# A fused attention and gated-linear kernel: three tiles' down products in one group, and stores, reloads and weight transfers placed anew

## The chip, the cores and the metric

The kernel runs on one core of a Trainium2 chip. A core has five instruction streams that run side by side and wait for one another by semaphores: TensorE (PE, with its weight loads shown apart as PEld), VectorE (DVE), ScalarE (ACT), GpSimd (POOL) and SyncE (SP). Each works through its own instructions in order. In this kernel nearly all transfers are issued by SP. The metric is the device time of one execution in microseconds; the time given is the median of several runs. One execution was also recorded by the hardware profiler; all rows quoted here come from such records, with times counted from the start of its span.

## The reference

The input x has 2048 rows of 512. Two blocks follow one another, each with a layer norm whose scale and shift come from a conditioning vector, and a gate on its result:

```python
x = x + ga * attention(layernorm(x) * (1 + ca) + sa)      # 32 heads, 4 segments of 512 rows, a memory from segment to segment
h = layernorm(x) * (1 + cb) + sb
g = h @ w_gate                                            # 512 x 1376
u = h @ w_up                                              # 512 x 1376
x = x + gb * ((g * u) @ w_down)                           # 1376 x 512
```

The change touches only the second block. The 1376 columns of g and u make eleven tiles: ten of 128 columns (numbers 0 to 9) and one of 96 (number 10, called LAST).

## The kernel before

The kernel works in single-precision inputs split into a high and a low part, so that a product takes three matmuls: high by high, low by high, high by low. In the code a pair of such parts is bH and bL (activations), cwH and cwL (gate and up weights), dH and dL (down weights), mH and mL (the product g * u). High parts are made by ACT with a copy, low parts by DVE with a subtraction.

The rows come in four segments of 512. The second block takes them in two passes: pass 0 has segments 0 and 1, pass 1 has segments 2 and 3. Within a pass the two segments are c = 0 and c = 1, and a segment has four row tiles t = 0 to 3.

**Two ways to do a tile.** Tiles 0, 1 and LAST of pass 0, and LAST of pass 1, are *plain*: `open0` multiplies the first half of the contraction for segment 0 (banks Xg and Xu) and keeps a copy q on ACT, `close0` adds the second half, and `other` does segment 1 (banks Yg and Yu), adding q to it. The other tiles go in pairs as *units*, one for g and one for u, which do a two-by-two block product with seven block multiplications instead of eight; their banks are X, Y and Z, and `build` prepares the sums of activation blocks that they need. `finish` takes what comes out: a copy gs on ACT for g, and for u the product on DVE followed by `split`, which makes mH on ACT and mL on DVE.

**Down products.** `down(p, fs, c, t)` multiplies the tiles in `fs` with their rows of w_down into one bank, acc, three matmuls to a tile, and adds the bank to the row tile xa on DVE (line 1344). For the tiles whose first is `ENDS[p]` the row tile is then complete: `down` issues its store to the output at once, and, in pass 0, the *reload* of the same buffer with the rows that pass 1 needs, at most three stores behind. `d` takes one down product out of the list `dq`; in the loop over units it is called between the steps of a unit, to give PE work while the others catch up.

**Kept weights.** Pass 0 loads and splits the weights of each tile and stores the split parts to device memory (`keep`, line 406); pass 1 fetches them (`fetch`, line 410) and has ACT copy them in place (line 416). `prepare(n)` is the generator that gets unit n's weights ready two units ahead. It is advanced step by step inside unit n - 1 (`old`), and for kept units started at step 4 of unit n - 2 (`pr`). There it fetches cwH and cwL; the fetches of the two down tiles come as later steps of the same generator, behind ACT's copies.

**What sets the order.** PE's instructions are chained in the order of the program. The other engines' orders come from a scheduler that works with its own estimate of times, so the order on ACT, DVE and SP can shift when the program order does. SP issues transfers in its order, and an issue whose buffer or data is not ready holds those behind it.

The stretch from the first plain tile to the unit loop is written out by hand, near the end of the kernel. `lg1` is the layer norm of segment 1; its last four steps are the 16 transposes of the normed rows (ctp) with ACT's scale and shift (chf, line 611). `xp`, `wdp` and `pr0` are the weights of tile LAST, the three plain down tiles (whose splits dHp and dLp share one buffer) and unit 0.

## Time and profile before

| | |
|---|---|
| time, median of 3 runs | 880.75 us (878.02 to 881.43) |
| the profiled execution's own time | 879.9 us |
| its span | 878.2 us |
| PE busy | 845.7 us, 96% |
| DVE busy | 655.6 us, 75% |
| ACT busy | 496.6 us, 57% |
| POOL busy | 274.4 us, 31%, nothing after about 520 us |
| moved by DMA | 141.29 MB, mean 161 GB/s |

The first block takes the span up to about 520 us; the plain tiles of pass 0 stand from 520 to 565, the units of pass 0 up to about 690, LAST of pass 1 up to about 706, and the units of pass 1 up to the end. A row of the timeline reads: start, length, engine, line, operation, output and inputs, shapes, count, and in brackets the idle time of the engine just before it with what ended it. Matmuls overlap and their ends are modelled, so that the distance from start to start says what one costs.

### The profile page before, as it was taken

To read this page: it belongs to the slowest core of one execution; us is meant where nothing else is said; L and a number is where in the kernel's file an instruction comes from. 1 tells how busy PE (TensorE), PEld (TensorE's weight loads), DVE (VectorE), ACT (ScalarE), POOL (GpSimd) and SP (SyncE) were. 2 spreads that over 40 slices of the span, in tenths; PEclk is the share of its full clock that TensorE was granted. 3 is DMA by queue.
4 is the path that set the end of the run, shared out by engine and by line. 5 is a ranking of instruction groups with operands and counts; after the bars stand their busy time and mean duration, and the time that the engine had idled before them with its cause. 6 is when DMAs were issued, how large, how long until landed. Compare 5 with 4: busy or idle time off the path is not lost.

```text
span 878.2 us, 14439 instructions
## 1 busy us (share of the span) xinstructions
PE 845.7 (96%) x4976; PEld 596.4 (68%) x4976; DVE 655.6 (75%) x1825; ACT 496.6 (57%) x755; POOL 274.4 (31%) x424
## 2 busy tenths in 40 slices
PE   8989999999999999999999999999999999999998
PEld 5755666565665565665665677877888777888886
DVE  7698777888778887788889358989796935546654
ACT  3757757677677685677544626343535745554420
POOL 4545535466546574575424610000000000000000
PEclk9999999999999999999999999999999999999999
DMA  7554443545536453557465448477742576342112
GB/s 236 154 162 123 122 120 100 172 129 172 132 88 184 119 149 113 132 165 227 147 202 188 143 167 311 162 247 281 254 178 84 199 240 229 148 175 89 49 49 96
DMA packets 83305, 141.29 MB, mean 161 GB/s; under 512 B 11712, under 2 KB 45504, under 8 KB 83232
## 3 DMA queue, kind: packets, MB, share of 16 engines
q1 hardware_dynamic: 83088, 140.35, 50.4%
q8 instruction: 39, 0.64, 0.3%
q14 instruction: 34, 0.28, 0.1%
q10 hardware_dynamic: 144, 0.02, 0.0%
HBM read 90.52 MB, written 49.55 MB: 160 GB/s over the span
## 4 chain that ended last, share of the span: by engine, by line
PE 75%; DVE 12%; ACT 6%; DMA 4%; issue 2%; POOL 1%; SPq 0%; ACTq 0%; POOLq 0%; DVEq 0%
PE acc L1341 14%; PE tb L85 8%; PE q L85 6%; PE k L85 6%; PE Xu L1274 5%; PE Xg L1274 5%; DVE q L39 5%; PE wops L85 5%; PE vps L85 4%; PE Yu L1274 4%; PE Yg L1274 4%; PE kps L85 3%; PE qps L85 3%; ACT pt L332 2%; PE Zu L1274 1%
## 5 line engine op out<-in xcount | busy, mean ns | idle before, releaser
L39 DVE CUSTOM_DVE_ANT_0 q<-q,cmask 128x384 f32<-128x384 f32 (+3 forms) x512 | 246.6, 508 | 49.7 <-PE q L85 39.6
L332 ACT ACTIVATE pt<-k 128x1024 f32<-128x1024 f32 x160 | 163.8, 1024 | 64.4 <-PE k L85 63.7
L338 POOL TENSOR_SCALAR_AFFINE_SELECT pt<-pt 128x256 f32<-128x256 f32 (+1 forms) x224 | 96.8, 446 | 166.1 <-ACT pt L332 163.7
L85 PE MATMUL q<-kst,qst 96*128 96x384 bf16 (+3 forms) x512 | 101.6, 299 | 11.4 <-DVE nm L39 9.8
L85 PE MATMUL k<-qst,kst 98*128 98x384 bf16 (+3 forms) x512 | 97.1, 302 | 5.0 <-ACT pt L332 4.9
L1344 DVE TENSOR_TENSOR xa<-xa,acc 128x512 f32<-128x512 f32 x96 | 65.6, 684 | 38.9 <-PE acc L1341 38.5
L85 PE MATMUL tb<-pt,v 128*32 128x512 f32 (+3 forms) x1024 | 75.5, 436 | 0.0
L39 DVE DVE_READ_ACCUMULATOR2_ANT nm<- 128x1 f32 x512 | 72.3, 141 | 0.0
L85 PEld LDWEIGHTS <-kst 98*128 98x128 bf16 x512 | 37.7, 98 | 49.5 <-issue 43.2
L85 PEld LDWEIGHTS <-qst 96*128 96x128 bf16 x512 | 43.1, 97 | 37.9 <-issue 14.1
L1341 PE MATMUL acc<-dH,mL 128*128 128x512 f32 (+1 forms) x152 | 60.0, 395 | 1.3 <-DVE mL L1294 1.3
L1341 PE MATMUL acc<-dH,mH 128*128 128x512 f32 (+1 forms) x152 | 60.3, 397 | 0.0
L1341 PE MATMUL acc<-dL,mH 128*128 128x512 f32 (+1 forms) x152 | 60.1, 395 | 0.0
L85 PEld LDWEIGHTS tb<-pt,v 128*32 128x32 f32 x1024 | 28.7, 109 | 38.6 <-issue 33.8
L364 ACT ACTIVATE tsb<-tb 128x512 f32<-128x512 f32 x32 | 19.0, 595 | 41.0 <-PE tb L85 41.0
L1341 PEld LDWEIGHTS acc<-dH,mL 128*128 128x128 f32 (+1 forms) x152 | 28.5, 188 | 8.4 <-DVE mL L1294 1.7
L1341 PEld LDWEIGHTS acc<-dL,mH 128*128 128x128 f32 (+1 forms) x152 | 28.6, 188 | 7.0
L1341 PEld LDWEIGHTS acc<-dH,mH 128*128 128x128 f32 (+1 forms) x152 | 28.5, 188 | 6.8
L1274 PE MATMUL Xu<-bH,cwH 128*128 128x512 f32 (+1 forms) x68 | 27.7, 407 | 3.2 <-DVE yu L1374 1.7
L85 PE MATMUL kps<-ahH,wkH 128*128 128x512 f32 x64 | 30.0, 469 | 0.0
L85 PE MATMUL wops<-woH,oH 128*128 128x512 f32 x64 | 28.3, 441 | 0.7 <-ACT oH L527 0.7
L85 PE MATMUL qps<-ahH,wqH 128*128 128x512 f32 x64 | 28.7, 448 | 0.0
(378 smaller groups left out, 2034.3 us busy)
## 6 DMA issues: line engine op xcount, KB each, us to landing
wm<-in_w_mod_dram SPq DMA_DIRECT2D x24, 256.0 KB, 4.4
kd<-k SPq DMA_DIRECT2D x16, 384.0 KB, 2.5
kst<-kd SPq DMA_DIRECT2D x32, 192.0 KB, 3.2
qd<-q SPq DMA_DIRECT2D x16, 384.0 KB, 3.1
qst<-qd SPq DMA_DIRECT2D x32, 192.0 KB, 3.6
x<-in_x_dram SPq DMA_DIRECT2D x16, 256.0 KB, 4.5
kst<-kd SPq DMA_DIRECT2D x32, 128.0 KB, 3.1
qst<-qd SPq DMA_DIRECT2D x32, 128.0 KB, 3.7
```

Of the source, the lines that this page charges most:

```text
L39: i = getattr(self.eng, name)(*a, **k)
L85: return pe(nc.tensor.matmul(*a, **k))
L332: ex = act.activation(pt, kp, AF.Exp, scale=0.25)
L338: sels[u, i] = nc.gpsimd.affine_select(w, w, pattern=[[0, w.shape[1]], [1, P]], compare_op=ALU.is_ge, fill=0.0, base=0, channel_multiplier=-1)
L364: act.activation(tsbs[u], tbs.pop(u), AF.Copy)
L1274: pe(nc.tensor.matmul(ps[0:n], a, b[:, k], start=first and c == 0, stop=last and c == 5, skip_group_check=True))
L1341: pe(nc.tensor.matmul(ps, a[0:m, t * P:(t + 1) * P], b[0:m], start=j == 0, stop=j == n - 1))
L1344: vec.tensor_add(xa, xa, ps)
```

## The change

There are four edits.

1. The down products of the plain tiles of pass 0 were two groups for each row tile, (0, 1) and (LAST,), thus two banks and two additions. They become one group `trio = (LAST, 0, 1)` of nine matmuls and one addition. For segment 0 the four groups stand together after `close0(0, LAST)`; for segment 1 four entries instead of eight go into `dq`, and unit 0 takes them at steps 1, 2, 4 and 6.
2. `run(lg1)`, segment 1's transposes, moves from after `close0(0, 0)` to after `open0(0, LAST)`; the first steps of `build` and of the down weights shift with it.
3. The store of a finished row tile of pass 0 is not issued by the down product that completes it but by the next one that does, and the reload that follows from it is later by as much. The first down product of pass 1 issues what is left.
4. For units with kept weights `prepare` issues all transfers (cwH, cwL, and for a u unit both pairs of down tiles; for the plain tile of pass 1 also its down tile) in its first step. ACT's copies follow step by step as before.

```diff
     def down(p, fs, c, t):
+        while p == 1 and outs and fs[0] != ENDS[1]:
+            store(0)
         while p == 1 and again:
             reload()
...
         if fs[0] == ENDS[p]:
-            nc.sync.dma_start(out[rows(2 * p + c, t), :], xa)
-            if p == 0:
-                again.append((c, t))
+            outs.append((c, t, xa))
+            if p == 1:
+                store(p)
+            else:
+                if len(outs) > 1:
+                    store(p)
                 if len(again) > 2:
                     reload()
+
+    outs = []
+
+    def store(p):
+        c, t, xa = outs.pop(0)
+        nc.sync.dma_start(out[rows(2 * p + c, t), :], xa)
+        if p == 0:
+            again.append((c, t))
...
         slot = -n % 3
+        if (nm, i) in wkeep:
+            gens = [(xprep if nm == "x" else wprep)(n, slot, pc, pc)]
+            gens += [wdprep(p, f) for f in {"g": (), "u": (i, i + 1), "x": (LAST,)}[nm]]
+            for g in gens:
+                next(g)
+            yield
+            for g in gens:
+                yield from g
+            return
...
     run(close0(0, 0))
-    run(lg1)
-    nb = build(0)
-    next(nb)
-    run(close0(0, 1))
     for w in wdp[:2]:
         next(w)
+    run(close0(0, 1))
     run(open0(0, LAST, qa[LAST]))
+    run(lg1)
     for w in wdp[:2]:
         next(w)
     next(wdp[2])
-    next(nb)
-    for t in range(2):
-        down(0, (0, 1), 0, t)
+    nb = build(0)
     next(nb)
     run(close0(0, LAST))
+    next(wdp[2])
     next(nb)
-    for t in range(2, 4):
-        down(0, (0, 1), 0, t)
+    trio = (LAST, 0, 1)
     for t in range(4):
         xload2(0, 1, t)
+    for t in range(4):
+        if t == 2:
+            next(nb)
+        down(0, trio, 0, t)
...
+    next(nb)
     for _ in other(0, LAST):
         next(pr0)
...
     for f in (0, 1):
-        for t in (2 * f, 2 * f + 1):
-            down(0, (LAST,), 0, t)
         for _ in other(0, f):
...
-    dq.extend(lambda f=f, t=t: down(0, f, 1, t) for f in ((LAST,), (0, 1)) for t in range(4))
+    dq.extend(lambda t=t: down(0, trio, 1, t) for t in range(4))
...
             if n == 0:
-                d(1 + st % 2 if st > 1 else 1)
+                d(st in (1, 2, 4, 6))
```

## The prediction

> **What bounds the kernel now.** I read the page first, then PE's waits over the second half, then the PE, ACT, DVE and SP timelines around each wait.

> ```profile
> span 878.2 us, 14439 instructions
> PE 845.7 (96%) x4976; PEld 596.4 (68%) x4976; DVE 655.6 (75%) x1825; ACT 496.6 (57%) x755; POOL 274.4 (31%) x424
> ```

> PE is busy for 96% of the span, and the change leaves every matmul in place: the compiled order has the same PE instructions in both kernels, and nothing in it differs ahead of the feed-forward part, at about 520 us. So only PE's pauses after 520 us can move. The PE timeline, where a bracket gives the idle time and its releaser, has these (rows from five places):

> ```profile
> 537.16 0.51 PE L1341 MATMUL acc<-dHp,mH 128*128 128x512 f32 x1 [0.51 <-ACT mH L1293]
> 537.89 0.51 PE L1341 MATMUL acc<-dHp,mL 128*128 128x512 f32 x1 [0.22 <-DVE mL L1294]
> 592.50 0.50 PE L1274 MATMUL Xu<-bH,cwH 128*128 128x512 f32 x1 [1.28 <-DVE yu L1374]
> 603.36 0.50 PE L1341 MATMUL acc<-dH,mL 128*128 128x512 f32 x1 [1.26 <-DVE mL L1294]
> 735.39 0.50 PE L1274 MATMUL Xu<-bH,cwH 128*128 128x512 f32 x1 [0.45 <-DVE yu L1374]
> 741.30 0.50 PE L1274 MATMUL Xu<-bH,cwH 128*128 128x512 f32 x1 [1.49 <-DVE p5u L1374]
> ```

> The brackets sum to 5.2 us. A bracket starts at the modelled end of the last matmul, which lies about 0.17 us after the next could have started, so each pause costs about that more: 1.2, 1.45, 1.45, 0.6 and 1.65 us, 6.3 us in all, 0.7% of the span. That is the ceiling of any gain, since the tail is untouched. A change under 0.5% (4.4 us) is about what a measurement of this kernel cannot tell from none, and the three runs shown spread by 3.4 us.

> **Part 1: grouping, and the transposes moved.** Eight down groups fewer mean eight DVE additions fewer, from this row 8 x 0.68 = 5.5 us of DVE.

> ```profile
> L1344 DVE TENSOR_TENSOR xa<-xa,acc 128x512 f32<-128x512 f32 x96 | 65.6, 684 | 38.9 <-PE acc L1341 38.5
> ```

> This is worth nothing in itself: its own idle time says that DVE waits 38.5 us for PE around these additions, and the two pauses that DVE does set after it, at 592 and 603 us, start from work that the change does not thin out. From the third weight split on (about 581 us) the DVE and ACT orders are alike in both kernels, and before it DVE waits for PE again:

> ```profile
> 586.39 0.69 DVE L1374 TENSOR_TENSOR p1u<-Zu,p1u 128x512 f32<-128x512 f32 x1 [1.23 <-ACT p1u L1394]
> 591.77 0.68 DVE L1374 TENSOR_TENSOR yu<-Xu,yu 128x512 f32<-128x512 f32 x1
> ```

> So DVE has no backlog at 586 us that fewer additions could shorten, and between 586 and 592 us it runs splits and products queued ahead of yu. I keep both pauses: 0.

> What costs is the order ahead of the first down product. Before, two down groups of tiles 0 and 1 stand between tile 2's two halves (open0 and close0 of LAST). After, the compiled order of PE is open0 of LAST, 16 transposes, close0 of LAST, then at once the grouped down products, which begin with LAST, the tile just finished. Nothing stands between to cover LAST's product and split. Rows for PE and ACT:

> ```profile
> 525.83 0.39 PE L1274 MATMUL Xg<-bh,gH 128*128 128x512 f32 x1
> 528.56 1.91 PE L88 MATMUL ctp<-ident,x 128*128 128x128 f32 x16
> 530.22 0.48 PE L1274 MATMUL Xg<-bh,gH 128*128 128x512 f32 x1
> ...
> 530.39 1.44 ACT L611 ACTIVATE chf<-ctp,modc 128x512 f32<-128x512 f32 x2
> 531.72 0.63 ACT L1310 ACTIVATE dHp<-crd 128x512 fp32r<-128x512 f32 x1
> 533.43 0.63 ACT L1230 ACTIVATE bH<-t 128x512 fp32r<-128x512 f32 x1
> 533.95 0.59 ACT L1365 ACTIVATE gs<-Xg 128x512 f32<-128x512 f32 x1
> 536.00 0.59 ACT L1441 ACTIVATE q<-Xu 96x512 f32<-96x512 f32 x1
> 536.49 0.62 ACT L1293 ACTIVATE mH<-gs 128x512 fp32r<-128x512 f32 x1
> 537.14 0.69 DVE L1294 TENSOR_TENSOR mL<-gs,mH 128x512 fp32r<-128x512 f32 x1 [0.94 <-ACT mH L1293]
> 542.91 0.68 DVE L1370 TENSOR_TENSOR gs<-gs,Xu 96x512 f32<-96x512 f32 x1 [0.54 <-ACT cwH L479]
> 563.10 1.29 DVE L1238 TENSOR_TENSOR t<-chf,chf 128x512 f32<-128x512 f32 x2
> ```

> Twelve matmuls take 2.73 us (525.83 to 528.56), the 16 transposes 1.66 (528.56 to 530.22). In the new order: close0 of tile 0 ends at 528.56, of tile 1 at 531.29, open0 of LAST at 534.02, the transposes at 535.68, close0 of LAST at 538.5 (0.1 for the restart after transposes). ACT, in its new order, copies the last open0 result until 534.75 (0.2 after its end, 0.53 to the next, as at 536.00), then has four chf (0.67 each, 1.33 for two in the row), one dHp (0.53), two bH (0.52 each) and only then the gate copy gs, at 539.0. The copy takes 0.6, the product on DVE 0.7, mH 0.65 with its handover: PE may start at 541.1. The low half mL follows 0.7 later, as 537.16 to 537.89 shows, against a matmul's 0.23, another 0.5. PE pauses 2.6 + 0.5 = 3.1 us where it paused 1.2. Cost 1.8. The ends: with ACT's copy of gs done early, Xu's end, product and mH alone leave 1.6 + 0.5, cost 0.9; with DVE slips of one more 0.6 us operation, 2.5. I take 1.8, because ACT's order is fixed and every link has a row.

> Later, at about 566 us, the six Y groups of 2.7 us now follow one another without down products between. DVE has 28 operations there, at 0.6 from start to start (the row at 563.10) under 16.8 us, and four of them are half as wide; PE needs 16.4 us, so DVE keeps up; the last tile's mL comes 0.7 us behind mH as above, with two thirds of the first grouped product (1.4 us) and a Z group (1.4 us) ahead of it. From Y's end: addition 0.7, mL of tile 0 0.6, product 0.6, mH 0.65, mL 0.7, or 3.25 us against 3.0 of cover: cost 0.25, from 0 to 1.

> **Part 2: kept transfers together, stores and reloads later.** The last two pauses begin on ACT, which waits in order for transfers that SP issued late:

> ```profile
> 724.54 0.69 DVE L1344 TENSOR_TENSOR xa<-xa,acc 128x512 f32<-128x512 f32 x1 [2.07 <-PE acc L1341]
> 722.88 0.38 SPq L1346 DMA_DIRECT2D out_dram<-xa  x1
> 726.55 0.38 SPq L410 DMA_DIRECT2D dH<-keptHd  x1
> 727.50 0.38 SPq L1346 DMA_DIRECT2D out_dram<-xa  x1
> 732.44 0.32 SPq L1321 DMA_DIRECT2D xa<-x1d  x1
> 732.87 0.37 SPq L410 DMA_DIRECT2D cwH<-keptHu  x1
> 731.11 0.63 ACT L416 ACTIVATE dH<-dH 128x512 fp32r<-128x512 f32 x1 [4.51 <-DMA dH<-keptHd]
> 734.65 0.69 DVE L1374 TENSOR_TENSOR yu<-Xu,yu 128x512 f32<-128x512 f32 x1
> 737.60 1.79 ACT L416 ACTIVATE cwH<-cwH 128x1024 fp32r<-128x1024 f32 x2 [3.70 <-DMA cwH<-keptHu]
> 740.56 0.68 DVE L1374 TENSOR_TENSOR p5u<-Xu,p5u 128x512 f32<-128x512 f32 x1
> 741.50 0.58 ACT L1394 ACTIVATE p5g<-Yg 128x512 f32<-128x512 f32 x1
> xa<-x1d SPq DMA_DIRECT2D x1, 256.0 KB, 9.9
> ```

> (The last row is the issue at 711.80, which stood behind two 896 KB fetches; its last column is us to landing.) SP sat from 727.50 to 732.44 on a reload whose store had not landed, with cwH queued behind it. In the new SP order the first pair of kept down tiles (dH, dL of tile 2) moves ahead of the second store, out of the way. Three of the last reloads come first, then dH and dL of tiles 3 and 4, the store, cwL and cwH, and the reload last.

> SP is the only queue touched; POOL and ACT issue none of these. At the first tiles SP also changes the order of stores of split weights, the second rows' x and one weight fetch; each is wanted 15 us or more after its issue, so 0.

> dH 3 is free when the last first-half product ends on PE (724.5), and the store ahead of it now follows its addition, not two reloads, so I put its issue at 724.9, not 726.55, and its landing 4.5 later at 729.4. ACT's gate copy, mH and the yu copy behind it follow 1.7 us sooner, yu on DVE at about 733, and PE is not held at 734.8: gain 0.6.

> The cw pair is issued when its slot comes free on PE (727.9) instead of at 732.9, 5 us sooner, but behind four down tiles and now with cwL first: I estimate cwH at 728.3 + 4.7 (its time alone, 732.9 to 737.6) + 2.7 for cwL (4.7 less a latency of 2) + 0.5 for what is left of the tiles, 736.2 against 737.6. Also mH of the waiting product now stands ahead of cwH in ACT's order. Then p5u need not wait for it, and the pause of 1.65 goes, as far as ACT is through with cwH and cwL (twice 1.79) and p5g by 740.4, when PE wants its bank. (Unheld, PE starts Xu at 734.8; Xu, Yg and Xg of 1.4 each bring it to the Xu that needs p5u at 739.05, and one more to 740.4.) 736.2 + 3.6 + 0.5 is 740.3. What is late next is thus ACT itself, and after it the last reload: its addition now stands directly ahead of p5u on DVE. Bounds of this part: gain 2.25, or a loss of 2.0 (below); I take a gain of 1.9, near the first, since issue times move only to the earlier side.

> Later kept units have the same SP, ACT and DVE order in both kernels and PE has no pause there; the tail is the same. The sum: +1.8 + 0.25 - 1.9 = +0.15 us on the profiled run's 879.9, which stands 0.85 under the median of 880.75. So 880.9 for a median.

> **Rivals.** *The clock falls in the new pause.* PE lost half its clock early in this run after a wait of 2.0 us and a stretch of one-column matmuls, and kept it after the 1.49 us wait at 741:

> ```profile
> 17.54 1.05 PE L85 MATMUL m<-ones,wm 128*128 128x1 f32 x8 [2.00 <-DVE wm L39]
> 19.00:20.00 1.00, 1.00 (x8) 0.86 (x7) 0.97 (x4) 0.00 (x0) 0.00 (x0) 0.83 0.00 0
> 20.00:21.00 1.00, 1.00 (x4) 0.81 (x3) 0.09 (x2) 0.79 (x2) 0.00 (x0) 0.50 0.42 129
> 23.00:24.00 1.00, 1.00 (x5) 0.58 (x3) 1.00 (x2) 0.73 (x3) 0.00 (x0) 0.96 0.00 0
> 741.00:744.00 3.00, 2.70 (x12) 2.22 (x13) 2.27 (x5) 2.64 (x5) 0.00 (x0) 1.00 0.10 27
> ```

> (In the windows the third number from the end is the granted clock.) The new pause of 2.6 us, one matmul, 0.5 us lies above the first wait. There the clock was halved from inside the slice at 19 to inside that at 23, some 3.4 us; the same here loses half of it, 1.7 us: 882.6. [...]

> *Slower: the last reload blocks DVE.* It is issued once its store has landed, about 732, behind cwL and cwH. If it takes the 9.9 us of the row above it lands at 741.9; the addition and p5u follow to 743.3, and PE, which wants p5u's bank at 739.05, pauses 4.25 us where it paused 2.25: Part 2 then costs 2.0 and the sum is 880.75 + 1.8 + 0.25 + 2.0 = 884.8. It decides from a landing at about 738; with a landing past 742.2, or with the clock's 1.7 beside it, the time passes 885.15, the 0.5% bound. Against it: the 9.9 us row was issued 1.3 us behind the pair, this reload would be 4 us behind. I expect 737.

> *Faster: the backlog argument is wrong,* and the DVE time saved removes the pauses at 592 and 603 (2.9 us), with Part 1 at its low end (0.9) and Part 2 at 2.25: 880.75 + 0.9 - 2.9 - 2.25 = 876.5; with another microsecond it would pass 876.35.

> *No effect in Part 2:* dH and cwH land no earlier because the four down tiles share the engines; then +2.05, 882.8.

> **Numbers.** Sum as worked out 0.45; half clock 0.2; no gain in Part 2 0.13; reload blocks 0.12; faster 0.1. The first three lie within 0.5%. Of the reload case I count all as slower, since a landing that late would likely be later still, and add 0.02 from the clock; of the faster case 0.08 as faster and 0.02 as within: 0.78, 0.14, 0.08. The range runs from the faster case's edge to a little past the reload case: 877 to 886. The likeliest case alone: 879 to 882.6.

> **What will show it.** PE's first matmul of the grouped product (acc from LAST's mH) should carry a bracket of about 2.4 us, its second 0.2 to 0.3. At about 594 and 605 the waits for yu and mL should stand as they do. At about 737 and 743 PE's waits for yu and p5u should be gone or under 0.5. Additions xa should be 88. The prediction fails if PE's first grouped product starts without a wait, if the granted clock in that stretch is 0.5, or if DVE's longest wait before p5u is for a transfer of xa.

## The result, and the profile after

In 20 runs of each on one chip the changed kernel took 882.59 us (881.06 to 884.24) and the kernel before 879.66 us (876.61 to 882.19): a ratio of 1.0034, with a 95% interval of 1.0025 to 1.0044. That is 3.0 us more, inside the 0.5% within which the prediction said "no change", but clear of zero: with 20 runs of each, a third of a per cent can be told from none. The page of the profiled execution, whose own time was 883.86 us:

```profile
span 882.1 us, 14432 instructions
PE 849.2 (96%) x4976; PEld 599.9 (68%) x4976; DVE 652.5 (74%) x1817; ACT 497.1 (56%) x755; POOL 274.6 (31%) x424
```

PE has the same 4976 matmuls and is busy 3.5 us longer, DVE has its eight operations fewer. How much of it lies in the feed-forward part is seen in the PE timeline, from the first gate product to the last down product. The first pair of rows is of the kernel before, the second of the changed one:

```profile
520.37 0.39 PE L1274 MATMUL Xg<-bh,gH 128*128 128x512 f32 x1
873.90 0.40 PE L1341 MATMUL acc<-dL,mH 128*128 128x512 f32 x1
```

```profile
521.03 0.39 PE L1274 MATMUL Xg<-bh,gH 128*128 128x512 f32 x1
877.88 0.40 PE L1343 MATMUL acc<-dL,mH 128*128 128x512 f32 x1
```

353.53 us became 356.85, 3.3 us more. This length is used below beside the medians, since it leaves out the attention part, which varies from execution to execution. Where it was lost, in PE's timeline of the changed kernel (rows from five places):

```profile
541.80 0.51 PE L1343 MATMUL acc<-dHp,mH 96*128 96x512 f32 x1 [2.50 <-ACT mH L1293]
542.52 0.58 PE L1343 MATMUL acc<-dHp,mL 96*128 96x512 f32 x1 [0.22 <-DVE mL L1294]
542.89 0.63 PE L1343 MATMUL acc<-dLp,mH 96*128 96x512 f32 x1
543.32 0.63 PE L1343 MATMUL acc<-dHp,mH 128*128 128x512 f32 x1
...
546.26 0.40 PE L1343 MATMUL acc<-dHp,mL 96*128 96x512 f32 x1
...
572.19 0.49 PE L1343 MATMUL acc<-dHp,mH 128*128 128x512 f32 x1 [0.29 <-ACT mH L1293]
572.91 0.50 PE L1343 MATMUL acc<-dHp,mL 128*128 128x512 f32 x1 [0.23 <-DVE mL L1294]
...
597.72 0.50 PE L1274 MATMUL Xu<-bH,cwH 128*128 128x512 f32 x1 [1.28 <-DVE yu L1387]
608.56 0.50 PE L1343 MATMUL acc<-dH,mL 128*128 128x512 f32 x1 [1.27 <-DVE mL L1294]
744.50 0.50 PE L1274 MATMUL Xu<-bH,cwH 128*128 128x512 f32 x1 [0.23 <-DVE p5u L1387]
746.46 0.50 PE L1274 MATMUL Yg<-bH,cwH 128*128 128x512 f32 x1 [0.30 <-ACT p5g L1407]
```

Two things are to be seen at 542 us. The first is a stand, a time in which PE starts nothing, of 2.50 and 0.22 us in brackets. The second has no bracket: from 542.89 to 546.26 us eight matmuls take 3.37 us, 0.42 each and not 0.23. Windows of the same trace, with PE's busy time first and the granted clock as the third number from the end:

```profile
539.40:542.80 3.40, 0.79 (x2) 0.47 (x3) 2.71 (x5) 2.45 (x6) 0.00 (x0) 1.00 1.05 404
542.80:546.20 3.40, 3.40 (x9) 2.63 (x9) 0.94 (x3) 0.81 (x2) 0.00 (x0) 0.50 0.70 255
546.20:549.60 3.40, 3.40 (x16) 2.77 (x16) 3.09 (x6) 0.00 (x0) 0.00 (x0) 1.00 0.00 0
```

PE did 9 matmuls in 3.4 us at half clock, where it does 16 at full clock.

The table sums, place by place, how much later than 0.2275 us after its forerunner each matmul started (0.1 us after a transpose; differences under 0.04 us left out). It is worked out from the PE timelines of each profiled execution, and has all the kernels of the next section. "Ahead of the first group" is the stretch from 535 to 548 us, half clock included; the fillers of e3 and e10 (1.8 and 0.9 us of matmuls) are work and not in it.

| kernel | ahead of the first group | about 570 us | about 593 and 604 us | about 735 to 748 us | from first gate product to last matmul |
|---|---|---|---|---|---|
| before | 1.28 | 0 | 3.2 | 2.47 | 353.53 |
| after | 5.00 | 1.07 | 3.2 | 1.08 | 356.85 |
| e1, Part 2 alone | 1.28 | 0 | 3.2 | 0.65 | 351.76 |
| e2, Part 1 alone | 5.01 | 1.06 | 3.2 | 1.67 | 357.29 |
| e3, 8 fillers | 1.58 | 1.07 | 3.2 | 1.04 | 355.10 |
| e10, 4 fillers | 4.10 | 1.07 | 3.2 | 1.03 | 356.66 |
| e4, last tile last | 3.61 | 1.06 | 3.2 | 1.81 | 356.05 |
| e5, transposes as cover | 1.07 | 0.90 | 3.2 | 0.30 | 351.93 |
| e6, later stores alone | 1.28 | 0 | 3.2 | 0.34 | 351.34 |
| e7, kept together alone | 1.28 | 0 | 3.2 | 0.80 | 351.84 |
| e8, combined | 0.15 | 0.60 | 3.2 | 1.46 | 351.86 |
| e9, e8 without kept together | 0.15 | 0.59 | 3.2 | 0.92 | 351.25 |

The length is that of one execution each. Set against before, it differs from what the times of all runs say by up to 1.7 us (e5: 1.6 us less by the length, nothing by the time). So the table shows where time went, and what a version is worth is read from its times.

Of the 5.00 us ahead of the first group 3.3 are the stand (2.66 + 0.49, and 0.14 at the third matmul) and 1.7 the half clock. The changes sum to +3.7 + 1.1 - 1.4 = +3.4 us, against 3.3 by the length.

### The profile page after: what moved, and what is told of

Its sections match the earlier page's. It is cut to its first block, busy times and chain, and to the rows that moved or that the text cites. A ratio compares the mean times of both kernels' runs of the same rounds, so it can differ in the third digit from the quotient of the medians.

```text
span 882.1 us, 14432 instructions
## 1 busy us (share of the span) xinstructions
PE 849.2 (96%) x4976; PEld 599.9 (68%) x4976; DVE 652.5 (74%) x1817; ACT 497.1 (56%) x755; POOL 274.6 (31%) x424
## 4 chain that ended last, share of the span: by engine, by line
PE 76%; DVE 13%; ACT 6%; DMA 2%; issue 2%; POOL 1%; SPq 0%; DVEq 0%; POOLq 0%
PE acc L1343 14%; PE tb L85 8%; PE q L85 6%; PE Xg L1274 6%; PE k L85 6%; PE Xu L1274 6%; DVE q L39 5%; PE wops L85 5%; PE vps L85 4%; PE Yu L1274 4%; PE Yg L1274 4%; PE kps L85 4%; PE qps L85 2%; ACT pt L332 2%; PE Zu L1274 1%
## 5 line engine op out<-in xcount | busy, mean ns | idle before, releaser
L39 DVE CUSTOM_DVE_ANT_0 q<-q,cmask 128x384 f32<-128x384 f32 (+3 forms) x512 | 246.6, 508 | 49.4 <-PE q L85 39.2
L85 PE MATMUL q<-kst,qst 96*128 96x384 bf16 (+3 forms) x512 | 101.6, 299 | 11.1 <-DVE nm L39 9.8
L85 PE MATMUL k<-qst,kst 98*128 98x384 bf16 (+3 forms) x512 | 97.1, 302 | 5.0 <-ACT pt L332 4.9
L1346 DVE TENSOR_TENSOR xa<-xa,acc 128x512 f32<-128x512 f32 x88 | 60.2, 684 | 45.5 <-PE acc L1343 42.5
L85 PE MATMUL tb<-pt,v 128*32 128x512 f32 (+3 forms) x1024 | 75.5, 436 | 0.0
L39 DVE DVE_READ_ACCUMULATOR2_ANT nm<- 128x1 f32 x512 | 72.3, 141 | 0.0
L85 PEld LDWEIGHTS <-kst 98*128 98x128 bf16 x512 | 37.7, 98 | 49.5 <-issue 43.2
L85 PEld LDWEIGHTS <-qst 96*128 96x128 bf16 x512 | 43.1, 97 | 37.7 <-issue 13.7
L85 PEld LDWEIGHTS tb<-pt,v 128*32 128x32 f32 x1024 | 28.7, 110 | 38.5 <-issue 34.1
L85 PE MATMUL kps<-ahH,wkH 128*128 128x512 f32 x64 | 30.3, 473 | 0.0
L1274 PE MATMUL Xu<-bH,cwH 128*128 128x512 f32 (+1 forms) x68 | 27.6, 405 | 1.5 <-DVE yu L1387 1.3
L85 PE MATMUL wops<-woH,oH 128*128 128x512 f32 x64 | 28.3, 442 | 0.7 <-ACT oH L527 0.7
L85 PE MATMUL qps<-ahH,wqH 128*128 128x512 f32 x64 | 28.7, 449 | 0.0
## 6 DMA issues: line engine op xcount, KB each, us to landing
wm<-in_w_mod_dram SPq DMA_DIRECT2D x24, 256.0 KB, 4.5
x<-in_x_dram SPq DMA_DIRECT2D x16, 256.0 KB, 4.6
```

The lines of the kernel that those rows point to most:

```text
L39: i = getattr(self.eng, name)(*a, **k)
L85: return pe(nc.tensor.matmul(*a, **k))
L1274: pe(nc.tensor.matmul(ps[0:n], a, b[:, k], start=first and c == 0, stop=last and c == 5, skip_group_check=True))
L1346: vec.tensor_add(xa, xa, ps)
```

## The experiments

**The two parts, each alone (e1, e2).** e1 is the kernel before with edits 3 and 4, e2 the changed kernel without them.

> The kernel before with Part 2 alone: stores and reloads later, kept units' transfers together; grouping and transposes stay as before. By the trace of after (the pauses at 735 and 741 us gone, 0.5 and 0.6 us of new ones at 744.5 and 746.5): 1.4 us faster than before, 0.9984 of it, at most the 1.9 of the prediction. If Part 2 has no effect by itself (the prediction's rival): same as before within 0.3 us, with the two pauses moved elsewhere in the pass.

> The changed kernel without Part 2, so grouping and transposes alone. If the loss is all in these: before + 1.9 (longer pause ahead of the first grouped down product) + 1.65 (half clock for the 3.4 us behind it) + 1.0 (pause in the second half's close) = +4.5 us, 1.0051 of before, with the granted clock near 0.5 between 543 and 546 us and the pauses at 735 and 741 us there again. If the loss came from the two parts together (the clock a matter of that execution): +1.8 to +2.2 us and a clock of 1.00 there.

e1 measured 0.9983 of before (0.9972 to 0.9993; 877.78 us against 879.17), e2 1.0053 (1.0037 to 1.0069; 883.99 us): 1.5 us gained and 4.7 us lost, as the first theories said. Their sum, 3.2 us, is about the loss of the whole change. In e2's windows the half clock is there without Part 2:

```profile
538.60:542.00 3.40, 1.23 (x4) 0.83 (x5) 2.71 (x6) 2.45 (x6) 0.00 (x0) 0.99 1.05 397
542.00:545.40 3.40, 3.40 (x10) 2.61 (x9) 1.28 (x3) 0.37 (x2) 0.00 (x0) 0.51 0.44 157
```

One detail of e2's expectation failed: the pause at 735 us was not there again. One pause was left, in PE's timeline of e2:

```profile
744.48 0.50 PE L1274 MATMUL Xu<-bH,cwH 128*128 128x512 f32 x1 [1.40 <-DVE p5u L1374]
```

So behind Part 1 there was less for Part 2 to gain by the traces: 0.6 us (1.67 to 1.08), where alone it gained 1.8 (2.47 to 0.65). By the times it gained 1.7 us there (1.0053 to 1.0034), but the two intervals overlap, so this does not contradict the traces.

**The stand and the clock (e3, e10).** In the function `down` of the changed kernel:

```diff
         n = 3 * len(fs)
         j = 0
+        if p == 0 and c == 0 and t == 0 and len(fs) == 3:
+            for _ in range(8):          # e10: 4
+                pe(nc.tensor.matmul(ps, mids[0, 0, 0][0][:, 0:P], wds[0, 0][0], start=True, stop=True))
```

> The changed kernel with eight extra matmuls, whose result is overwritten, put into the pause ahead of the first grouped down product; nothing waits for less or for more. Theory A, the clock falls because TensorE stands still there: the pause shrinks from 2.66 us to about 0.9, the granted clock stays 1.00 from 542 to 547 us, and the whole is 1.65 us faster than the changed kernel although there is more to compute. Theory B, the clock falls for another reason (the mean load around there, or the grouped products themselves): the 3.4 us of half clock stay and the time is that of the changed kernel.

> The kernel of e3 with four extra matmuls in place of eight: the stand ahead of the first grouped down product is 2.66 - 0.9 = 1.75 us instead of 0.84, with 0.5 us at the second matmul unchanged. Theory A (about 3.4 us at half clock follow where TensorE stood for half or more of the 3.4 us before): 2.3 us of standing in 3.4, half clock for 3.4 us behind it in most executions, so 0.9 us slower than e3 by the longer pause less the shorter filler (0) plus up to 1.65 us of clock: the time of the changed kernel, 1.0034 of before. Theory B (only a stand of over 2.5 us in one piece brings it): full clock and the time of e3, 1.0017.

e3 took 1.0017 of before (1.0005 to 1.0029), 1.5 us less than the changed kernel, with eight matmuls more. PE's timeline and a window of e3:

```profile
539.23 2.00 PE L1340 MATMUL acc<-dHp,mH 128*128 128x512 f32 x8
541.89 0.50 PE L1346 MATMUL acc<-dHp,mH 96*128 96x512 f32 x1 [0.65 <-ACT mH L1293]
542.61 0.50 PE L1346 MATMUL acc<-dHp,mL 96*128 96x512 f32 x1 [0.22 <-DVE mL L1294]
```

```profile
542.80:546.20 3.40, 3.40 (x16) 2.77 (x16) 2.40 (x5) 0.91 (x3) 0.00 (x0) 1.00 0.56 201
```

The down product starts when it did (541.89 against 541.80), so nothing was released sooner; only the clock stayed at 1.00. That is theory A: the half clock follows from PE's standing still, and it costs about 1.6 us (1.5 by the times, 1.75 by the lengths). e10, with half the filler, took 1.0042 (1.0028 to 1.0056), as slow as the changed kernel:

```profile
540.77 0.50 PE L1346 MATMUL acc<-dHp,mH 96*128 96x512 f32 x1 [1.56 <-ACT mH L1293]
541.49 0.63 PE L1346 MATMUL acc<-dHp,mL 96*128 96x512 f32 x1 [0.22 <-DVE mL L1294]
```

```profile
541.80:545.20 3.40, 3.40 (x9) 2.65 (x9) 0.89 (x3) 0.79 (x2) 0.00 (x0) 0.51 0.48 171
```

Stands of 1.56 and 0.22 us by the brackets (1.74 and 0.49 by the starts) were enough. Theory B, that it takes over 2.5 us in one piece, is out. Theory A's "half or more" is an estimate: e4's stands (below; 1.26 + 0.49 us by the starts, half clock behind them) and e3's (0.84 + 0.49 us, full clock) lie on its two sides, and no run shows half itself.

**Ready operands first (e4).** The group of the changed kernel, in the first half alone, in another order:

```diff
-    trio = (LAST, 0, 1)
+    trio = (0, 1, LAST)
...
-    dq.extend(lambda t=t: down(0, trio, 1, t) for t in range(4))
+    dq.extend(lambda t=t: down(0, (LAST, 0, 1), 1, t) for t in range(4))
```

> The changed kernel, but in the first half the group goes through tiles 0, 1 and then the last, so that the down product begins with operands that are ready, and only its seventh matmul waits for the tile just closed. Theory A (length of the stand): six matmuls of 0.22 us cover 1.3 us of the 2.66 + 0.5, the stand is 1.8 us, the clock stays 1.00, 1.3 + 1.65 = 3.0 us faster than the changed kernel and so level with before. Theory B (the clock falls whatever the pause): 1.3 us faster than the changed kernel. Rival C: the operands of tiles 0 and 1 are late too and nothing is gained.

Measured 1.0022 (1.0008 to 1.0037): about 1.1 us less than the changed kernel, not 3.0, and so near theory B's number. In the profiled execution the stand shrank as worked out, and half clock still followed it:

```profile
542.11 0.50 PE L1343 MATMUL acc<-dHp,mH 96*128 96x512 f32 x1 [1.11 <-ACT mH L1293]
542.83 0.50 PE L1343 MATMUL acc<-dHp,mL 96*128 96x512 f32 x1 [0.22 <-DVE mL L1294]
```

```profile
540.50:543.90 3.40, 2.07 (x9) 1.15 (x8) 1.89 (x4) 2.47 (x5) 0.00 (x0) 0.99 1.04 386
543.90:547.30 3.40, 3.40 (x10) 2.63 (x9) 3.00 (x6) 0.03 (x1) 0.00 (x0) 0.50 0.25 89
```

I had taken a stand of 1.8 us as safe because the clock stays at 1.00 behind the old pauses of 1.45 us. It was not, at least in this execution. But this one, with 884.55 us, is the slowest of e4's twelve, and the clock did not fall in all of them: two have a granted clock of 0.999 over the whole execution, a loss of 0.9 us, and one stretch of 3.4 us at half clock alone would lose 1.7 (none of the twenty runs of the changed kernel has more than 0.998). So theory B, by which it falls whatever the pause, does not hold either. The section on the hardware comes back to this.

**The transposes as cover (e5).** In the changed kernel:

```diff
     run(open0(0, LAST, qa[LAST]))
-    run(lg1)
...
-    nb = build(0)
-    next(nb)
     run(close0(0, LAST))
+    run(lg1)
+    nb = build(0)
+    next(nb)
```

> The changed kernel with the second segment's norm transposes taken from ahead of the third tile's close and put behind it, ahead of the first grouped down product (the build that uses them follows them). Theory: the pause there is the time in which ACT and DVE finish the last tile, so 16 transposes of 0.1 us cover 1.6 us of the 2.66 us stand, 0.5 at the second matmul stays, the clock stays 1.00, and the time is 1.6 + 1.65 = 3.2 us below the changed kernel, level with before. Rival: the evictions of the transposes run ahead of the last tile's work on ACT and DVE, or the transposes wait for a bank, so that the down product comes as late as in the changed kernel: 0 to 1.6 us gained, and half clock perhaps again.

Measured 1.0001 (0.999 to 1.0013), 879.37 us: level with before, 2.9 us under the changed kernel's ratio, as the theory said. PE's and ACT's timelines and a window of e5:

```profile
537.41 1.91 PE L88 MATMUL ctp<-ident,x 128*128 128x128 f32 x16
539.39 0.49 PE L1343 MATMUL acc<-dHp,mH 96*128 96x512 f32 x1
540.20 0.50 PE L1343 MATMUL acc<-dHp,mL 96*128 96x512 f32 x1 [0.31 <-DVE mL L1294]
536.25 0.59 ACT L1378 ACTIVATE gs<-Xg 96x512 f32<-96x512 f32 x1 [0.76 <-PE Xg L1274]
```

```profile
540.40:543.80 3.40, 3.40 (x16) 2.73 (x16) 2.25 (x5) 3.40 (x7) 0.00 (x0) 1.00 1.05 396
```

The down product now starts 2.0 us after the first transpose, which comes straight behind the close, while in the changed kernel PE stood for 2.66 us there. With ACT freed of the four chf ahead of the gate copy, the operands come sooner as well: the copy starts at 536.25 us, 1.2 us before the close is done, and in the changed kernel at 539.57, 0.4 us after it. Grouping by itself thus costs nothing ahead of the first group (1.07 us against 1.28); what costs there is that the transposes were moved to where they load ACT and cover nothing.

**The two edits of Part 2 (e6, e7).** The kernel before with edit 3 alone, and with edit 4 alone, as the diff above shows them.

> The kernel before with the stores and reloads later, and nothing else. If this edit alone carries Part 2 (store and reload no longer stand ahead of the kept units' loads at 735 to 741 us): the two pauses there (0.6 and 1.65 us) shrink to 0.6 us in all, 1.5 to 1.8 us faster than before. If the kept units' transfers carry it: pauses and time as before.

> The kernel before with the kept units' transfers issued together, and nothing else. If this edit alone carries Part 2: the pauses at 735 and 741 us shrink from 2.25 us to about 0.6 us, 1.5 to 1.8 us faster than before. If the stores carry it: as before, within 0.3 us; if both are needed, each alone brings under half of it.

e6 took 0.998 of before (0.9966 to 0.9994; 877.38 us), e7 0.9993 (0.998 to 1.0005). By the traces each alone takes most of the pauses away, from 2.47 us to 0.34 and 0.80, which is e7's first expectation too; its time followed by about a third of that (0.6 us). By the traces the two edits are not parts of one gain but two ways to the same one: together they leave 0.65 us (e1), no less than the later stores alone. What is left in e7, in PE's timeline:

```profile
741.22 0.50 PE L1274 MATMUL Xu<-bH,cwH 128*128 128x512 f32 x1 [0.54 <-DVE p5u L1374]
```

By the times only e6's gain is settled; e7's interval takes in no change.

**All together (e8, e9).** e8 is e5 with e4's order, and with the second half's first grouped product one step later; e9 is e8 without edit 4.

```diff
             if n == 0:
-                d(st in (1, 2, 4, 6))
+                d(st in (2, 3, 4, 6))
```

> The changed kernel with the transposes behind the third tile's close, the group going through tiles 0, 1 and then the last in the first half, and in the second half the first grouped down product one step later (steps 2, 3, 4, 6 of the first unit in place of 1, 2, 4, 6). Theory: 1.6 us of transposes and 1.3 us of six ready matmuls cover the whole 2.66 + 0.5 us, so no pause and full clock at 540 us; the pause at 572 us (1.0 us) goes too. In the trace's time from the first gate product to the end: 356.85 - 3.1 - 1.65 - 1.0 = 351.1 us against 353.5 of before and 351.8 with Part 2 alone, so 2.4 us faster than before, some 0.997 of it. Rival: the finish of the last tile is put later by the evictions of the transposes on ACT and DVE, and 1 us of pause stays: 352 us and the same time as with Part 2 alone.

> The kernel of e8 with the kept units' transfers as before, so with the later stores and reloads as the only thing left of Part 2. Theory, from e6 and e7 (the later stores alone leave 0.2 us of pauses at 735 to 742 us, the transfers together alone leave 0.7 us): the 1.1 us of pauses that e8 shows at 740 to 742 us fall to about 0.3 us, 0.8 us faster than e8, 0.998 of before. Rival, the two pauses come from the earlier start of the whole pass: they stay, and the time is that of e8 (0.999).

e8 measured 0.999 (0.9977 to 1.0004), e9 0.9985 (0.9974 to 0.9996; 878.84 us). Ahead of the first group the pause is gone (0.15 us). e8 was to gain 2.4 us and gained 1.7 by the length and 0.9 by the time, with an interval that takes in no change and leaves out the expected 0.997. Two places kept what was to go: at 570 us the half that comes with mL stays (0.60 us), and at 740 us there are 1.46 us, where the changed kernel has 1.08. Leaving edit 4 out lowered this to 0.92 us in e9's trace, not to the expected 0.3; by the times e8 and e9 cannot be told apart. The pauses at 740 us in PE's timeline of e8:

```profile
739.89 0.50 PE L1274 MATMUL Xu<-bH,cwH 128*128 128x512 f32 x1 [0.52 <-DVE p5u L1387]
741.84 0.50 PE L1274 MATMUL Yg<-bH,cwH 128*128 128x512 f32 x1 [0.29 <-ACT p5g L1407]
```

Three versions beat both kernels, e6, e1 and e9, and their intervals overlap. The simplest is e6: the kernel before with the later stores and nothing else, 1.8 us faster.

## Why the prediction was right, and where it was wrong

The forecast of 880.9 us was no change within 0.5%, by a sum of +0.15 us. No change by that bound it was, and 882.59 lies in the range, but only because bound and range are wide: the sum was too low by some 3 us. The case that came was the first rival, half clock in the new pause, which had 0.2 of the chance and a time of 882.6. That this time is met almost exactly is luck: the rival adds 1.85 us to a before of 880.75, the runs show 2.9 us on a before of 879.66, and the median of the first three runs lay 1.1 us above that of the twenty, as much as the rest of the sum was too low.

Of the three signs of failure that the prediction names, two came: the granted clock was 0.50 in that stretch, and DVE's longest wait there ahead of p5u, 2.28 us, was for a transfer of xa.

- **Eight additions fewer, worth 0:** right. There are 88 of them, and DVE's idle time ahead of them is longer than before, 45.5 us, of which 42.5 for PE (38.9 and 38.5 before):

```profile
L1346 DVE TENSOR_TENSOR xa<-xa,acc 128x512 f32<-128x512 f32 x88 | 60.2, 684 | 45.5 <-PE acc L1343 42.5 <-DMA xa<-x1d 2.3
```

- **The pauses at 592 and 603 us kept:** right, 1.28 and 1.27 us in the brackets at 597.72 and 608.56, in all twelve traces alike. The faster rival is out.
- **The new pause ahead of the first group, 3.1 us:** right, and link by link. The chain was put to start PE at 541.1 us; the changed kernel reached its first gate product 0.66 us later than before, and the down product at 541.80 is 541.14 on the old count. The links, in ACT's and DVE's timelines of the changed kernel:

```profile
539.57 0.60 ACT L1378 ACTIVATE gs<-Xg 96x512 f32<-96x512 f32 x1
540.40 0.68 DVE L1383 TENSOR_TENSOR gs<-gs,Xu 96x512 f32<-96x512 f32 x1
541.12 0.63 ACT L1293 ACTIVATE mH<-gs 96x512 fp32r<-96x512 f32 x1 [0.95 <-DVE gs L1383]
```

- **Full clock behind it:** wrong, and the step of the prediction that failed. The sum left the clock at 1.00 and gave half clock 0.2, though the row at 17.54 us (2.00 us of waiting, then half clock) had spoken for it, and against it only a shorter wait of 1.49 us, behind which the clock stayed at 1.00. That it would stay so behind 2.6 us was an estimate that no row of before shows. The price put on it, 1.7 us, was what it cost.
- **0.25 us at about 566 us, from 0 to 1:** mis-sized; it measured 1.07 us. Rows 572.19 and 572.91 are 0.46 and 0.49 us late by their starts. The chain added up DVE's work and mH's own time, but not ACT's order. DVE's and ACT's timelines of the changed kernel:

```profile
570.34 0.69 DVE L1383 TENSOR_TENSOR q<-q 128x512 f32<-128x512 f32 x1
570.46 1.15 ACT L1230 ACTIVATE bH<-t 128x512 fp32r<-128x512 f32 x2 [2.22 <-DVE mL L1294]
571.52 0.61 ACT L1293 ACTIVATE mH<-q 128x512 fp32r<-128x512 f32 x1
```

The product is there at 571.0, but two copies for the next unit stand ahead of mH on ACT, and it starts 0.5 us later; mL follows it by 0.7. e8 shows the cover that is lacking: with the group one step later, the part that mH caused goes and mL's stays.
- **Part 2, a gain of 1.9 us:** right by itself (e1: 1.8 us of pauses, 1.5 us of time), too much for the whole, where the traces have 1.4 us less than before at that place and only 0.6 less than e2. The queue moved as said: the cw pair was put at 728.3 us, and its second half stands at 733.45, 728.25 on the old count (5.2 us less by the rows at 603.36 and 608.56). But cwH landed nine microseconds later, not eight, and the reload shortly behind it. The latency of 2 us in the sum for cwH is an estimate: of before's transfers the quickest kinds land, in the median, 1.7 us (qst from nt, 4 KB) and 2.0 us (the stores out of xa, 256 KB) after their issue, and no run shows it for cwL. SP's, ACT's and DVE's timelines of the changed kernel:

```profile
733.45 0.38 SPq L410 DMA_DIRECT2D cwH<-keptHu  x1
735.86 0.32 SPq L1321 DMA_DIRECT2D xa<-x1d  x1
742.46 1.79 ACT L416 ACTIVATE cwH<-cwH 128x1024 fp32r<-128x1024 f32 x2 [2.91 <-DMA cwH<-keptHu]
745.84 0.57 ACT L1407 ACTIVATE p5g<-Yg 128x512 f32<-128x512 f32 x1
743.16 0.69 DVE L1346 TENSOR_TENSOR xa<-xa,acc 128x512 f32<-128x512 f32 x1 [2.28 <-DMA xa<-x1d]
743.76 0.68 DVE L1387 TENSOR_TENSOR p5u<-Xu,p5u 128x512 f32<-128x512 f32 x1
```

These are the late transfers behind the two pauses left, and the two things that the prediction named as late next: ACT with p5g (cwH at 737.3 on the old count, 736.2 predicted) and the reload ahead of p5u (738.0; 737 predicted, 738 given as the point from which it decides).

Put together: +0.15 of the sum, +1.7 of clock, +0.8 at 570 us, +0.5 at 740 us and +0.2 at the first group make 3.4, against 3.3 by the length.

## What to carry to other kernels

When work is moved away from between two dependent steps, price the pause that opens and the clock behind it together: here a pause 2 us longer cost 3.7. Before grouping, ask which operand of the group is finished last, put it last, and keep work of another kind (here the transposes) between its making and its use. And test two edits that aim at one wait one by one: here, by the traces, each took most of it, and both together no more.

## What the runs showed of the hardware

```profile
591.00:594.40 3.40, 2.12 (x9) 1.60 (x9) 3.40 (x7) 1.03 (x3) 0.00 (x0) 1.00 1.07 392
601.00:604.40 3.40, 2.14 (x10) 1.44 (x9) 3.40 (x9) 1.46 (x4) 0.00 (x0) 1.00 0.83 257
741.40:744.80 3.40, 3.40 (x15) 2.80 (x16) 2.46 (x4) 2.45 (x6) 0.00 (x0) 1.00 0.27 91
```

Each of these is one execution. e4's clock did not fall every time (0.999 over the whole execution in two of twelve); why is not shown, since only one execution of each kernel has a trace.

In the changed kernel's trace the granted clock changes, up to the last matmul, at 17.14, 23.96, 542.79 and 546.20 us: half clock for 6.82 us, full clock for 518.83 us, half clock for 3.41 us. The long stretch at full clock:

```profile
23.96:542.79 518.83, 496.90 (x3448) 320.97 (x3447) 404.99 (x1372) 342.58 (x499) 263.88 (x388) 1.00 0.53 154
```

PE's busy time, whose ends are modelled, tells the cases apart less well: e4 has 2.07 us of it from 540.50 to 543.90 us and half clock next, the kernel before 1.99 us from 739.88 to 743.29 us and full clock next. At the start of the run it tells nothing: in e7's trace the clock falls between 14.50 and 15.00 us, behind 3.42 us of busy time from 11.00 to 14.50 us.

**The start of the run is a source of spread.** Between 14 and 26 us the traces differ, though the kernels are alike there: e6 has no half clock, before, e9 and e10 have 3.4 us of it, the changed kernel 6.8 us, and e5, e7 and e8 have 10.2 us. A stretch of e6 and of e7:

```profile
18.00:21.00 3.00, 2.74 (x18) 2.13 (x17) 2.02 (x6) 1.17 (x3) 0.00 (x0) 1.00 0.18 53
```

```profile
18.00:21.00 3.00, 3.00 (x15) 3.00 (x16) 1.86 (x5) 0.92 (x2) 0.00 (x0) 0.50 0.03 5
```

e6's first gate product starts at 519.76 us and e7's at 521.96, 2.2 us later. How much of that is the clock was not measured by itself; it is as large as most effects studied here, which is why the lengths from the first gate product were read beside the medians.
